# Hash attention and a squared-ReLU layer: the general path's transfers on GpSimd's queue, its flag loaded inside the last output product, and the last block's quarters turned by VectorE alone

## The chip, the cores and the metric

The kernel runs on one core of a Trainium2 chip. The metric is the device time of one execution in microseconds. A core has a matrix engine (TensorE, PE in the profile), three engines for elementwise work (VectorE or DVE, ScalarE or ACT, GpSimd or POOL) and SyncE (SP), which mostly issues transfers. Each engine runs its own queue of instructions in order and waits on semaphores that others raise. DMA queues move data between the main memory (HBM) and the on-chip memory (SBUF); matmuls write to PSUM. SP, ACT and POOL can issue transfers.

## The reference

```python
def _attn_ref(q, k, v, proj):                 # q, k, v: (4, 8, 768, 64), proj: (64, 6)
    scale = 1.0 / np.sqrt(D)
    q_bits = (np.einsum('bhsd,dk->bhsk', q, proj) > 0).astype(np.int64)
    k_bits = (np.einsum('bhsd,dk->bhsk', k, proj) > 0).astype(np.int64)
    powers = 2 ** np.arange(n_bits)
    q_bucket = np.sum(q_bits * powers, axis=-1)
    k_bucket = np.sum(k_bits * powers, axis=-1)
    mask = q_bucket[:, :, :, None] == k_bucket[:, :, None, :]
    scores = scale * np.matmul(q, k.transpose(0, 1, 3, 2))
    scores = np.where(mask, scores, -1000000000.0)
    scores = scores - np.max(scores, axis=-1, keepdims=True)
    attn = np.exp(scores)
    attn = attn / (np.sum(attn, axis=-1, keepdims=True) + 1e-09)
    return np.matmul(attn, v).astype(np.float32)

def _moe_ref(x, w_in, w_out):                 # x: (3072, 512), w_in: (512, 2048), w_out: (2048, 512)
    h = x @ w_in
    r = np.maximum(h, 0.0)
    return ((r * r) @ w_out).astype(np.float32)
```

The attention's heads are joined to 512 features per token and go through the second function. Everything is float32.

## The kernel before

The program has two paths. The **fast path** (up to line 1454) does the whole work without taking the maximum of the scores out first. The **general path** (`general`, line 1459) computes everything again in the safe way, in loops; it is skipped unless the inputs are large. Which it is, is decided by a flag, `slow`: the kernel squares and sums all of q and k in 32 pieces (`load_peak`, `peak`), `tops` (line 886) and `guard` (line 889) take the largest sum, and `guard` writes `slow` (line 895) as 1 if it is over a bound. At the end every engine loads `slow` into a register (line 1488) and branches (line 1489). For the inputs of the metric the flag is 0 and the general path isn't run.

The fast path has two stages. The first does attention, two heads at a time. The second does both weight matrices with a scheme that saves multiplications: a 2x2 block product takes seven products of sums of blocks instead of eight, and it is used twice, one inside the other. Tokens are worked in three chunks of 1024 (`NCHUNK`). Of a chunk, the hidden layer comes first (`hidden`, `hidden_pair`), then `project(i)` (line 1258) makes the output with seven outer products, k = 0 to 6, each of them a call of `product` (line 828).

One call of `product` in `project` is seven groups of four fp32 matmuls (a group is one call of the inner function `add`), over three accumulators in PSUM. The trace shows each of these matmuls as two, so a group is 8 rows. ScalarE copies snapshots of the accumulators to SBUF between the groups (`one`, `two`, `five`, `three`, by `keep`, line 844), and the callbacks c11, c12, c21, c22 combine them on VectorE (line 1199) into blocks of the output. I number the groups 0 to 6 in the order of the code. Group 2 starts in the accumulator of group 0 once `one` has been copied; `two` waits for group 2, `five` for group 3, `three` for group 4; c11 needs group 1, c22 needs `three` and `five`, c12 group 5, c21 group 6. `hook` is called after group 1 and puts VectorE's preparation of later operands there.

The order of the work is that of the code: each engine takes its instructions as the program emits them. `guard` is emitted after the product k = 5 of the last chunk and before the last product, k = 6. Its transpose on PE (line 892) is queued right ahead of group 0 of the last product; its two small VectorE instructions (lines 894, 895) are queued behind all the combining and turning of product 5.

The output's blocks are held with features along the partitions and have to be turned before they are stored. `put_out` (line 1209) turns 32x32 squares on VectorE and stores the block in four transfers with 128 bytes in a run. The last product of the last chunk makes one block row in four quarters, n = 0, 3, 1, 2 in that order (`last` moves c22 ahead of c12), each 128x256. `close` sends quarters 0, 3 and 1 to `put_part` (line 1225): VectorE turns the 32x32 squares, and four transfers of 32 KB go out, two on GpSimd's queue and two on SP's. Quarter 2, the last, goes to `put_last` (line 1240): PE transposes its two 128x128 halves into PSUM, VectorE copies one half and ScalarE the other to SBUF, and each half goes out in one transfer of 64 KB, on SP's and on ScalarE's queue.

After that come the loads of the flag, the branches, and an end section: SP waits for the semaphores of all transfers and engines, and two barriers follow. In the general path all transfers are issued from SP's queue, and two from ScalarE's; the loops over heads, query tiles, batches and so on are real loops with registers.

Of the kernel before, what the change touches and what calls it, by code (L numbers as in the profile page):

```python
# [8 lines left out]
FP32 = mybir.dt.float32  # L9
# [25 lines left out]
def kernel(  # L35
# [10 lines left out]
    nc = tc.nc  # L46
# [3 lines left out]
    NBITS = proj.shape[1]  # L50
    DM = H * D
    DFF = moe_w_in.shape[1]
    P = 128
# [12 lines left out]
    NCH = 1024  # L66
    NCHUNK = B * S // NCH
# [3 lines left out]
    ident = glob.tile([P, P], FP32, name="ident")  # L71
    slow = glob.tile([1, 1], I32, name="slow")
# [584 lines left out]
    with tc.manual_schedule():  # L657
# [166 lines left out]
        )  # L824

        KEPT = dict(one=2, two=1, three=2, five=1)

        def product(n, w, at, bt, c11, c12, c21, c22, hook=None, last=False):

            acc = [ps_m.tile([P, 512], FP32, name=f"acc{i}")[:, 0:w] for i in range(3)]

            def add(to, a, b, first, last):
                for i in range(n):
                    nc.tensor.matmul(  # L837
                        out=acc[to], lhsT=a(i), rhs=b(i), start=first and i == 0,
                        stop=last and i == n - 1, skip_group_check=True,
                    )  # L840

            def keep(of, name):
                t = p_r.tile([P, 512], FP32, name=name, bufs=KEPT[name])[:, 0:w]
                nc.scalar.copy(out=t, in_=acc[of])  # L844
                return t

            add(0, at(0), bt["11"], True, False)
            one = keep(0, "one")
            add(1, at(1), bt["21"], True, True)
            if hook:  # L850
                hook()
            c11(acc[1], one)
            add(0, at(4), bt["t2"], False, False)
            two = keep(0, "two")
            add(2, at(3), bt["t1"], True, False)
            five = keep(2, "five")
            add(0, at(5), bt["t3"], False, False)
            three = keep(0, "three")
            add(2, at(6), bt["22"], False, True)
            if last:  # L860
                c22(three, five)
            c12(acc[2], two)
            if not last:
                c22(three, five)
            add(0, at(2), bt["t4"], False, True)
            c21(acc[0])
# [372 lines left out]

        def put_last(n, o):  # L1240

            row, col = n // 2, n % 2
            ot = p_r.tile([P, HN], FP32, name="h", bufs=NH)[:, 0:QN]
            lo = (NCHUNK - 1) * NCH + col * QN
            for t in range(QN // P):
                at = slice(t * P, (t + 1) * P)
                tp = ps_m.tile([P, 512], FP32, name=f"acc{t}")[:, 0:P]
                nc.tensor.transpose(out=tp, in_=o[:, at], identity=ident)  # L1248
                if t:
                    nc.scalar.copy(out=ot[:, at], in_=tp)  # L1250
                else:
                    nc.vector.tensor_copy(out=ot[:, at], in_=tp)
# [202 lines left out]

    general(tc, slow, ident, w_in_7, w_in_21, w_out_1, q, k, v, proj, out_v)


def general(tc, slow, ident, w_in_7, w_in_21, w_out_1, q, k, v, proj, out_v):


    nc = tc.nc
# [16 lines left out]
    with ExitStack() as stack:  # L1479
# [7 lines left out]
        y_dram = drams.tile([NFF, P, S], FP32, name="y_d")  # L1487
        flag = nc.values_load(slow)
        with tc.If(flag > 0), ExitStack() as inner:
# [3 lines left out]
            for n, f, c in (0, 0, 0), (5, nf, 0), (6, nf, nr):  # L1493
                for i in range(nf):
                    nc.sync.dma_start(
                        out=w_in_d[c:c + nr, :, f + i], in_=w_in_7[:, :, n, i]
                    )
            for i in range(nf):
                nc.sync.dma_start(
                    out=w_in_d[nr:NFF, :, i].rearrange("r p c -> p r c"),  # L1500
                    in_=w_in_21[:, i].rearrange("p (r c) -> p r c", c=P),
                )
            nc.sync.dma_start(out=w_out, in_=w_out_1)
            pool = inner.enter_context(tc.tile_pool(name="g_pool", bufs=1))
# [21 lines left out]
            with tc.For_i(0, B * H, 1) as hd:  # L1526
                nat = []
                for i, src in enumerate(heads):
                    t = pool.tile([P, SB * D], FP32, name=f"g_nat{i}")
                    nc.sync.dma_start(  # L1530
                        out=t, in_=src[bass.ds(hd, 1)].rearrange("o p f -> (o p) f")
                    )
# [17 lines left out]
                )  # L1550
                nc.sync.dma_start(
                    out=ext_dram.rearrange("t r c -> r t c"),
                    in_=ext[0:K, 0].rearrange("r (t c) -> r t c", t=SB),
                )
                with tc.For_i(0, SB, 1) as qt:
                    ext_q = pool.tile([P, P], FP32, name="g_ext_q")
                    nc.sync.dma_start(
                        out=ext_q[0:K], in_=ext_dram[bass.ds(qt, 1)].rearrange("o r c -> (o r) c")
# [29 lines left out]
                    for t in range(SB):  # L1588
# [8 lines left out]
                    )  # L1597
                    nc.sync.dma_start(
                        out=x_dram[bass.ds(hd, 1)][:, bass.ds(qt, 1)].rearrange("o u p d -> (o u p) d"),
# [4 lines left out]
            with tc.For_i(0, B, 1) as b:  # L1604
                with tc.For_i(0, NFT, 1) as j:
                    x_nat = pool.tile([P, SB, 2, D], FP32, name="g_xn")
                    for h in range(2):
                        nc.sync.dma_start(
                            out=x_nat[:, :, h],
                            in_=xs[bass.ds(b * NFT + j, 1), :, :, h].rearrange("o p t d -> (o p) t d"),  # L1610
                        )
                    x_j = pool.tile([P, S], FP32, name="g_xj")
                    turn(x_j, [x_nat[:, t].rearrange("p h d -> p (h d)") for t in range(SB)], P)
                    nc.sync.dma_start(
                        out=xt_dram[bass.ds(j, 1)].rearrange("o p s -> (o p) s"), in_=x_j
                    )
                x_t = pool.tile([P, NFT, S], FP32, name="g_xt")
                nc.sync.dma_start(out=x_t, in_=xt_dram.rearrange("j p s -> p j s"))
                with tc.For_i(0, NFF, 1) as ff:
                    w = pool.tile([P, NFT, P], FP32, name="g_w")  # L1620
                    nc.sync.dma_start(
                        out=w, in_=w_in_d[bass.ds(ff, 1)].rearrange("o p t c -> (o p) t c")
                    )
                    for c in range(2):
                        hp = ps.tile([P, 512], FP32, name="g_hp")
                        for ft in range(NFT):
# [7 lines left out]
                        nc.vector.tensor_tensor(out=r, in0=r, in1=r, op=ALU.mult)  # L1634
                        nc.sync.dma_start(
                            out=y_dram[bass.ds(ff, 1), :, c * HS:(c + 1) * HS].rearrange(
# [4 lines left out]
                with tc.For_i(0, SB, 1) as t:  # L1641
                    gate = pool.tile([P, NFF, P], FP32, name="g_gate")
                    nc.sync.dma_start(
                        out=gate,
# [5 lines left out]
                    for ff in range(NFF):  # L1650
# [5 lines left out]
                    nc.scalar.copy(out=o, in_=y)  # L1656
                    nc.sync.dma_start(
                        out=out_v[bass.ds(b, 1)][:, bass.ds(t, 1)].rearrange("o u p m -> (o u p) m"),
# [31 lines left out]
```

## Time and profile before

| what | us |
|---|---|
| median of 3 runs (lowest, highest) | 860.94 (860.58, 861.04) |
| the profiled execution | 861.34 |
| its span, first to last instruction | 859.6 |
| PE busy | 847.7 |
| VectorE busy | 748.8 |
| ScalarE busy | 401.9 |
| GpSimd busy | 169.0 |
| granted clock of PE, mean of the span | 0.997 |

The span is what the trace shows; 1.74 us of the profiled execution's time lie around it. PE is busy 99% of the span, so the other engines' busy times matter only where PE waits for them. Loads of registers, branches, waits on semaphores and the issuing of transfers aren't counted as busy; they are found in the view of one line's instructions and in the waits of a queue (SPq is SP's queue, PEldq PE's sequencer). Line numbers are those of the kernel before; in the changed kernel the same code stands 1 line (in `product`) to 18 lines further up or down.

### The profile page before, as it was taken

Reading aid. Unit: us, or ns where it says so; the run is one execution under the profiler, and the core shown is the slowest. Engines: PE = TensorE matmul, PEld = TensorE weight load, DVE = VectorE, ACT = ScalarE, POOL = GpSimd, SP = SyncE. Lnnn points to the kernel's source line nnn. Section 1 sums busy time; section 2 is a strip of 40 time slices with the busy share of each in tenths; the row PEclk is TensorE's granted clock in tenths of the full one; section 3 lists DMA queues with packets and bytes.
Section 4 is the critical chain, followed back from the end, with each engine's and each line's share of the span. In section 5 each row is a group of like instructions: output and inputs, shape, how many; then the busy total and the mean of one; then the engine's idle time right before and its main releaser. Section 6 shows DMA issues by size and latency. Waiting matters only on the chain.

```text
span 859.6 us, 17003 instructions
## 1 busy us (share of the span) xinstructions
PE 847.7 (99%) x6593; PEld 528.6 (62%) x6593; DVE 748.8 (87%) x1026; ACT 401.9 (47%) x752; POOL 169.0 (20%) x284
## 2 busy tenths in 40 slices
PE   8999999999999999999999999999999999999996
PEld 3544444444544444444788866567888766668885
DVE  5899999999999987988979978888889788888875
ACT  5787777788877752222111145553111355541110
POOL 1321111123221101643122121111000211100004
PEclk9999999999999999999999999999999999999998
DMA  9677898879998526999977975538557865335565
GB/s 202 134 145 152 175 187 197 198 165 257 246 228 218 169 69 234 326 319 302 346 241 224 268 184 203 182 98 298 174 158 197 178 217 187 122 119 158 159 168 117
DMA packets 235175, 170.15 MB, mean 198 GB/s; under 512 B 168552, under 2 KB 192176, under 8 KB 235088
## 3 DMA queue, kind: packets, MB, share of 16 engines
q1 hardware_dynamic: 195376, 87.85, 41.4%
q0 software_dynamic: 16608, 42.54, 16.1%
q10 hardware_dynamic: 23104, 38.61, 14.8%
q8 instruction: 53, 0.87, 0.4%
q14 instruction: 34, 0.28, 0.1%
HBM read 127.14 MB, written 41.16 MB: 196 GB/s over the span
## 4 chain that ended last, share of the span: by engine, by line
PE 98%; DMA 1%; DVE 0%; ACT 0%; issue 0%; ACTq 0%; DVEq 0%
PE acc L837 41%; PE st L430 18%; PE xo L485 14%; PE acc L1097 13%; PE acc L1050 8%; PE tot L534 2%; PE hash L360 1%; DMA qk_nat<-in_k_dram 1%; ACT e L436 0%; DVE bits L410 0%; PE xo L360 0%; DVE feat L329 0%; PE tp L320 0%; ACTq L284 0%; PE acc L1248 0%
## 5 line engine op out<-in xcount | busy, mean ns | idle before, releaser
L436 ACT ACTIVATE e<-st 128x768 f32<-128x768 f32 x192 | 155.4, 810 | 59.0 <-PE st L430 56.1
L430 PE MATMUL st<-feat 64*64 64x384 f32 x1536 | 157.8, 483 | 1.0 <-DVE feat L329 1.0
L485 PE MATMUL xo<-e,v_nat 64*64 64x385 f32 (+1 forms) x1520 | 157.6, 483 | 0.0
L837 PE MATMUL acc<-b,leaf 128*128 128x256 f32 x600 | 133.2, 379 | 0.4 <-issue 0.4
L837 PEld LDWEIGHTS acc<-b,leaf 128*128 128x128 f32 x600 | 113.8, 190 | 16.8 <-issue 1.3
L473 DVE TENSOR_TENSOR total<-total,e 128x1536 f32<-128x1536 f32 x64 | 111.7, 1745 | 4.2 <-ACT e L436 2.8
L396 POOL DMA_DIRECT2D bits<-signed x120 | 61.9, 520 | 217.8 <-ACT signed L385 199.2
L485 PEld LDWEIGHTS xo<-e,v_nat 64*64 64x64 f32 (+1 forms) x1520 | 57.2, 133 | 66.5 <-issue 57.6
L1097 PE MATMUL acc<-t_x,w_unit 128*128 128x512 f32 x192 | 90.9, 595 | 0.0
L430 PEld LDWEIGHTS st<-feat 64*64 64x64 f32 x1536 | 56.4, 133 | 38.6 <-issue 33.0
L837 PE MATMUL acc<-t,leaf 128*128 128x256 f32 x336 | 76.0, 379 | 0.0
L837 PEld LDWEIGHTS acc<-t,leaf 128*128 128x128 f32 x336 | 63.8, 190 | 8.9 <-issue 0.3
L912 DVE SCALAR_TENSOR_TENSOR b<-h 128x512 f32<-128x512 f32 x96 | 65.7, 691 | 3.0
L430 PE MATMUL st<-bits 64*64 64x384 bf16 x768 | 65.4, 325 | 0.5 <-ACT e L436 0.3
L837 PE MATMUL acc<-x,w_unit 128*128 128x512 f32 x128 | 56.5, 593 | 0.0
L837 PE MATMUL acc<-b_t,leaf 128*128 128x256 f32 x240 | 53.8, 379 | 0.0
L844 ACT COPY two<-acc 128x256 f32<-128x256 f32 (+1 forms) x29 | 12.5, 431 | 87.8 <-PE acc L837 53.8
L1097 PEld LDWEIGHTS acc<-t_x,w_unit 128*128 128x128 f32 x192 | 35.8, 190 | 26.7 <-issue 23.0
L1218 POOL DMA_DIRECT2D out_dram<-h x24 | 15.5, 655 | 182.0 <-DVE h L1213 180.4
L837 PEld LDWEIGHTS acc<-b_t,leaf 128*128 128x128 f32 x240 | 45.5, 190 | 6.3
L844 ACT COPY one<-acc 128x256 f32<-128x256 f32 (+1 forms) x29 | 12.5, 432 | 78.8 <-PE acc L837 64.3
L430 PEld LDWEIGHTS <-bits 64*64 64x64 bf16 x768 | 24.1, 107 | 38.1 <-issue 37.4
(178 smaller groups left out, 1288.9 us busy)
## 6 DMA issues: line engine op xcount, KB each, us to landing
leaf<-w_out ACTq DMA_DIRECT2D x142, 256.0 KB, 3.1
raw<-in_moe_w_in_dram SPq DMA_DIRECT2D x8, 1024.0 KB, 6.9
raw<-in_moe_w_out_dram SPq DMA_DIRECT2D x8, 1024.0 KB, 7.8
w_unit<-w_in SPq DMA_DIRECT2D x16, 512.0 KB, 4.1
w_unit<-w_in SPq DMA_DIRECT2D x8, 896.0 KB, 8.6
w_out<-sums POOLq DMA_DIRECT2D x16, 448.0 KB, 7.6
v_nat<-in_v_dram SPq DMA_DIRECT2D x16, 384.0 KB, 5.2
x_all<-x_t SPq DMA_DIRECT2D x16, 384.0 KB, 3.0
```

Of the source, the lines that this page charges most:

```text
L396: nc.gpsimd.dma_start(out=t[h * D:h * D + NBITS + 1, w, c * HS:(c + 1) * HS], in_=signed[at:at + NBITS + 1, h],)
L430: nc.tensor.matmul(out=st[k * HK:(k + 1) * HK, h, 0:HS], lhsT=src[1][rows, key], rhs=src[0][rows, cut], start=first, stop=not first, skip_ ...
L436: nc.scalar.activation(out=key_of(pr, kt)[:, :, i, 0:HS], in_=st[:, :, 0:HS], func=ACTF.Exp, scale=scale)
L473: nc.vector.tensor_tensor(out=totals[pr], in0=totals[pr], in1=e, op=ALU.add)
L485: return nc.tensor.matmul(out=outs[pr][h * D:(h + 1) * D, c, 0:HS + 1], lhsT=nat[pr, "v_nat"][rows, h, kt * D:(kt + 1) * D], rhs=key_of(pr ...
L534: done = nc.tensor.matmul(out=spares[pr][g * 32:(g + 1) * 32, c2, 0:QS], lhsT=ones[rows], rhs=totals[pr][rows, h, c, c2 * QS:(c2 + 1) * QS ...
L837: nc.tensor.matmul(out=acc[to], lhsT=a(i), rhs=b(i), start=first and i == 0, stop=last and i == n - 1, skip_group_check=True,)
L844: nc.scalar.copy(out=t, in_=acc[of])
L912: nc.vector.scalar_tensor_tensor(out=out, in0=h, scalar=0.0, in1=h, op0=ALU.max, op1=ALU.mult)
L1050: nc.tensor.matmul(out=out, lhsT=w(a), rhs=b, start=start, stop=stop, skip_group_check=True)
L1097: nc.tensor.matmul(out=to, lhsT=w[:, PLACE[a], f], rhs=bt[b](f), start=first and f == 0, stop=last and f == NFT // 2 - 1, skip_group_check ...
L1218: queue.dma_start(out=out[at, m0 + a * 32:m0 + (a + 1) * 32].rearrange("(c i) j -> i c j", i=32), in_=ot[a * 32:(a + 1) * 32].rearrange("i ...
```

## The change

Three things are changed.

1. In the last product, right after c11 (behind group 1 on PE), `nc.values_load(slow)` is called. It puts one load of the flag on the queue of each of the five engines: on PE between groups 1 and 2, on ScalarE ahead of the copy `two`, on VectorE behind the turning of quarter 0, on SP and GpSimd behind the stores of quarter 0. Each load waits until VectorE has written `slow`. The register is handed to `general`, which branches on it and loads no flag of its own.
2. `put_last` and the table `LATE` are gone. All four quarters of the last block go through `put_part`: VectorE turns 32x32 squares, and four transfers of 32 KB go out, two on SP's queue and two on ScalarE's, for quarter 0 on GpSimd's.
3. In `general`, every transfer is issued from GpSimd's queue instead of SP's and ScalarE's.

```diff
+        flags = []
         KEPT = dict(one=2, two=1, three=2, five=1)
@@ product
             c11(acc[1], one)
+            if last:
+                flags.append(nc.values_load(slow))
             add(0, at(4), bt["t2"], False, False)
             two = keep(0, "two")
@@ put_part
-        LATE = {0: (nc.gpsimd, nc.sync), 3: (nc.sync, nc.gpsimd), 1: (nc.sync, nc.gpsimd)}
-
             for a in range(P // 32):
-                LATE[n][a % 2].dma_start(
+                queue = (nc.sync, nc.scalar if n else nc.gpsimd)[a % 2]
+                queue.dma_start(
                     out=out[lo:lo + QN, m0 + a * 32:m0 + (a + 1) * 32].rearrange(
                         "(c i) j -> i c j", i=32
                     ),
                     in_=ot[a * 32:(a + 1) * 32].rearrange("i (c j) -> i c j", j=32),
-                )
-
-        def put_last(n, o):
-
-            row, col = n // 2, n % 2
-            ot = p_r.tile([P, HN], FP32, name="h", bufs=NH)[:, 0:QN]
-            lo = (NCHUNK - 1) * NCH + col * QN
-            for t in range(QN // P):
-                at = slice(t * P, (t + 1) * P)
-                tp = ps_m.tile([P, 512], FP32, name=f"acc{t}")[:, 0:P]
-                nc.tensor.transpose(out=tp, in_=o[:, at], identity=ident)
-                if t:
-                    nc.scalar.copy(out=ot[:, at], in_=tp)
-                else:
-                    nc.vector.tensor_copy(out=ot[:, at], in_=tp)
-                (nc.scalar if t else nc.sync).dma_start(
-                    out=out[lo + t * P:lo + (t + 1) * P, HD + row * P:HD + (row + 1) * P],
-                    in_=ot[:, at],
                 )
@@ close
                 if (i, ih, jh) == (NCHUNK - 1, 1, 0):
-                    put = put_last if n == 2 else put_part
-                    put(n, o[0][:, n % 2 * QN:(n % 2 + 1) * QN])
+                    put_part(n, o[0][:, n % 2 * QN:(n % 2 + 1) * QN])
@@
-    general(tc, slow, ident, w_in_7, w_in_21, w_out_1, q, k, v, proj, out_v)
+    general(tc, flags[0], ident, w_in_7, w_in_21, w_out_1, q, k, v, proj, out_v)
@@ general
-        flag = nc.values_load(slow)
         with tc.If(flag > 0), ExitStack() as inner:
...
-                    nc.sync.dma_start(
+                    nc.gpsimd.dma_start(
                         out=w_in_d[c:c + nr, :, f + i], in_=w_in_7[:, :, n, i]
                     )
...
-                nc.scalar.dma_start(out=projx[:, c * NBITS:(c + 1) * NBITS], in_=proj)
+                nc.gpsimd.dma_start(out=projx[:, c * NBITS:(c + 1) * NBITS], in_=proj)
```

The rest of the diff is the same replacement of `nc.sync.dma_start` in `general` by `nc.gpsimd.dma_start`, thirteen more times.

More of the change, by code (lines that the diff above doesn't have):

```diff
@@ L1454, with general @@
     fast.close()
-    general(tc, slow, ident, w_in_7, w_in_21, w_out_1, q, k, v, proj, out_v)
-def general(tc, slow, ident, w_in_7, w_in_21, w_out_1, q, k, v, proj, out_v):
+    general(tc, flags[0], ident, w_in_7, w_in_21, w_out_1, q, k, v, proj, out_v)
+def general(tc, flag, ident, w_in_7, w_in_21, w_out_1, q, k, v, proj, out_v):
     nc = tc.nc
@@ L1498, in general @@
             for i in range(nf):
-                nc.sync.dma_start(
+                nc.gpsimd.dma_start(
                     out=w_in_d[nr:NFF, :, i].rearrange("r p c -> p r c"),
@@ L1502, in general @@
                 )
-            nc.sync.dma_start(out=w_out, in_=w_out_1)
+            nc.gpsimd.dma_start(out=w_out, in_=w_out_1)
             pool = inner.enter_context(tc.tile_pool(name="g_pool", bufs=1))
@@ L1529, in general @@
                     t = pool.tile([P, SB * D], FP32, name=f"g_nat{i}")
-                    nc.sync.dma_start(
+                    nc.gpsimd.dma_start(
                         out=t, in_=src[bass.ds(hd, 1)].rearrange("o p f -> (o p) f")
@@ L1550, in general @@
                 )
-                nc.sync.dma_start(
+                nc.gpsimd.dma_start(
                     out=ext_dram.rearrange("t r c -> r t c"),
@@ L1556, in general @@
                     ext_q = pool.tile([P, P], FP32, name="g_ext_q")
-                    nc.sync.dma_start(
+                    nc.gpsimd.dma_start(
                         out=ext_q[0:K], in_=ext_dram[bass.ds(qt, 1)].rearrange("o r c -> (o r) c")
@@ L1597, in general @@
                     )
-                    nc.sync.dma_start(
+                    nc.gpsimd.dma_start(
                         out=x_dram[bass.ds(hd, 1)][:, bass.ds(qt, 1)].rearrange("o u p d -> (o u p) d"),
@@ L1607, in general @@
                     for h in range(2):
-                        nc.sync.dma_start(
+                        nc.gpsimd.dma_start(
                             out=x_nat[:, :, h],
@@ L1613, in general @@
                     turn(x_j, [x_nat[:, t].rearrange("p h d -> p (h d)") for t in range(SB)], P)
-                    nc.sync.dma_start(
+                    nc.gpsimd.dma_start(
                         out=xt_dram[bass.ds(j, 1)].rearrange("o p s -> (o p) s"), in_=x_j
@@ L1617, in general @@
                 x_t = pool.tile([P, NFT, S], FP32, name="g_xt")
-                nc.sync.dma_start(out=x_t, in_=xt_dram.rearrange("j p s -> p j s"))
+                nc.gpsimd.dma_start(out=x_t, in_=xt_dram.rearrange("j p s -> p j s"))
                 with tc.For_i(0, NFF, 1) as ff:
                     w = pool.tile([P, NFT, P], FP32, name="g_w")
-                    nc.sync.dma_start(
+                    nc.gpsimd.dma_start(
                         out=w, in_=w_in_d[bass.ds(ff, 1)].rearrange("o p t c -> (o p) t c")
@@ L1634, in general @@
                         nc.vector.tensor_tensor(out=r, in0=r, in1=r, op=ALU.mult)
-                        nc.sync.dma_start(
+                        nc.gpsimd.dma_start(
                             out=y_dram[bass.ds(ff, 1), :, c * HS:(c + 1) * HS].rearrange(
@@ L1642, in general @@
                     gate = pool.tile([P, NFF, P], FP32, name="g_gate")
-                    nc.sync.dma_start(
+                    nc.gpsimd.dma_start(
                         out=gate,
@@ L1656, in general @@
                     nc.scalar.copy(out=o, in_=y)
-                    nc.sync.dma_start(
+                    nc.gpsimd.dma_start(
                         out=out_v[bass.ds(b, 1)][:, bass.ds(t, 1)].rearrange("o u p m -> (o u p) m"),
```

## The prediction

> **What bounds the kernel now.** I read the page's chain of waits first: PE carries 98% of the span, so whatever holds PE is paid in full, and whatever another engine does costs only after PE's last matmul.
>
> ```profile
> PE 98%; DMA 1%; DVE 0%; ACT 0%; issue 0%; ACTq 0%; DVEq 0%
> ```
>
> Then the timeline of the last 20 us, PE alone and then the rows beside it (start, length, engine, line, operation, out<-in, count):
>
> ```profile
> 839.45 3.62 PE L837 MATMUL acc<-b_t,leaf 128*128 128x256 f32 x16
> 842.90 3.62 PE L837 MATMUL acc<-t,leaf 128*128 128x256 f32 x16
> 846.36 5.34 PE L837 MATMUL acc<-b_t,leaf 128*128 128x256 f32 x24
> 852.21 0.44 PE L1248 MATMUL acc<-ident,o 128*128 128x128 f32 x2 [0.51 <-DVE o L1199]
> ```
>
> ```profile
> 844.47 0.71 DVE L1213 STREAM_TRANSPOSE h<-o 128x512 f32<-128x512 f32 x1
> 845.10 0.24 DVE L894 TENSOR_REDUCE most<-tp 1x1 f32<-1x128 f32 x1
> 845.37 0.14 DVE L895 TENSOR_SCALAR slow<-most 1x1 int32<-1x1 f32 x1
> ...
> 851.74 0.42 DVE L1199 TENSOR_TENSOR o<-sum,acc 128x256 f32<-128x256 f32 x1 [0.36 <-PE acc L837]
> 852.58 0.29 DVE L1252 COPY h<-acc 128x128 f32<-128x128 f32 x1 [0.42 <-PE acc L1248]
> ```
>
> The last product is the 56 matmul rows of PE from 839.45: seven groups of 8, 12.1 / 7 = 1.73 us each. Group 1 (the second) is done and group 2 starts at 842.90. VectorE is behind: it writes `slow` at 845.37 + 0.14 = 845.51, **2.6 us after PE went on to group 2**. Nothing on PE waits for `slow` today. PE ends at 851.70, the span at 859.6: a tail of 7.9 us. What fills it is in the view of one line's instructions (the load of the flag, L1488; the branch, L1489) and in the waits of SP's queue:
>
> ```profile
> L1488 PEldq TENSOR_LOAD <-slow x1: 487/487/487, 852.2 to 852.2; - x1
> L1488 DVEq TENSOR_LOAD <-slow x1: 645/645/645, 852.6 to 852.6; - x1
> L1488 SPq TENSOR_LOAD <-slow x1: 516/516/516, 853.3 to 853.3; - x1
> ...
> L1489 SPq EVENT_SEMAPHORE  x8: 17/17/17, 857.4 to 857.9; - x8
> ```
>
> ```profile
> SPq L1489 <- SPq L1489: 3.4, 1, 3.4
> ```
>
> SP issues the last store at 852.9, loads the flag, branches at 853.9 over the untaken general path and runs nothing for 3.4 us. No transfer explains it: the last stores issue at 852.90 and 852.98 and need 3.5 and 3.6 us to land (view of L1253), so they are down by 856.5, while SP's first check, of a transfer that landed earlier, comes at 857.4. PE, DVE and ACT go on 0.4 to 0.5 us after the same branch. In the built program SP jumps 269 instructions, POOL 156, ACT 169, DVE 189. The page's queue of instruction loads for these four (q14) carries 0.28 MB in 34 packets, 8.2 KB each; all instruction packets together are 1.15 MB for 17,003 instructions, 68 bytes each, so a packet is some 120 instructions. I read SP's 3.4 us as a jump past what had been loaded, with a load to wait for.
>
> **The change, part by part.**
>
> *Flag loaded early.* The load on PE now stands between groups 1 and 2 and waits for `slow`. PE's queue is in order: in the trace PE's load, whose flag had been there since 845.51, ran only at 852.21, when the weight load ahead of it was released. So groups 2 to 6 are queued behind it, and VectorE, ScalarE and the stores behind those. Price: flag 845.51, load 0.49, 0.1 to the next instruction (the gap between PE's load and its branch), weights 0.2: group 2 starts at 846.35 instead of 842.90, **+3.45 us**. If the load lets the next instruction pass, 845.75, +2.85; the order of rows says it holds, so I take 3.45. The flag cannot come sooner: VectorE's rows from 837.88 to 845.51 stand back to back, and the diff moves nothing ahead of L895. The other four loads are hidden: ACT's 0.60 lies before the copy `two`, which waits 3.1 us for PE; DVE's 0.65 before `tmp` of quarter 3, which waits 0.77 us for a copy, and longer after the stall; SP's 0.52 and POOL's 0.54 before a store not due for 1.3 us, or before nothing.
>
> *PE's clock.* PE then idles from 843.1 to 846.35, 3.25 us. This trace has no such gap. The rows nearest to it (columns: stretch, length, PE busy, PEld, DVE, ACT, POOL, granted clock, DMA share, GB/s):
>
> ```profile
> 850.65:854.06 3.41, 1.49 (x7) 0.77 (x5) 1.40 (x4) 0.27 (x1) 2.01 (x4) 1.00 0.63 106
> 854.06:857.40 3.34, 0.00 (x0) 0.00 (x0) 0.00 (x0) 0.00 (x0) 0.00 (x0) 0.50 0.10 25
> ...
> 4.14:7.56 3.42, 2.34 (x15) 1.21 (x14) 0.00 (x0) 0.86 (x2) 0.00 (x0) 1.00 1.47 167
> ```
>
> The records have full clock from 4.14 to 854.06, 249 times 3.413 us, so it is decided on a fixed grid. After a stretch with PE busy 1.49 of 3.41 us (44%) it was halved; after one with 2.34 (68%) it was not. A gap of 3.25 us puts at least 1.6 us of idling into one stretch, so that stretch is at most 52% busy; on this grid (843.82 to 847.23) 26%. I expect half clock for one stretch: of 0.9 to 1.7 us of lost work, by where the grid falls, I take **+1.6**; ends 0 and 3.4 (two stretches).
> The Trainium skill, "TensorE: Matmul & The Clock Gate", Part 1, says that the clock halves after at least one idle window of about 3.4 us, free-running. The grid agrees with the trace; the 44% row speaks against "idle". By the Trainium skill's wording a gap of 3.25 us fills no window, and the sum would lack the 1.6.
>
> *The tail.* Removed: PE's two transposes (0.44), both copies, all five flag loads, POOL's four late stores. Added: VectorE's transpose of 128x256, 0.45 (L1229). With PE's end still at 851.70: `o` to 852.17, transpose to 852.66 (today's copies end at 852.87 and 852.96). Then two stores each on SP and ACT, 0.32 and 0.45 to issue. SP's second shares a semaphore with ACT's first store of quarter 1 (issued about 851.4, landing 1.8 later), so it goes at 853.25, ends 853.7 and lands at 855.05, by the 1.8 us of the median of such SP stores. SP jumps at 853.75, over 169 instructions instead of 269: as ACT did over 169 in 0.5 us. After the landing come what is left of the semaphore checks and the barrier, 1.2 us in today's rows (858.4 to 859.6). End 856.25; 0.3 more for instruction loads of other engines in the way (I put today's 3.5 us of the last stores down to them: five such packets in 853.5 to 855.8), 856.6: **-3.0 us**. Bounds: -3.3, and -0.8 if SP still waits for instructions.
> The Trainium skill, "Runtime: NRT & Kernel Launch", Instruction fetch mechanics, has a taken branch out of a two-block window wait for a load, as I read SP's row; its blocks are 256 instructions, against the 120 of q14 here. With its blocks SP's 269 would mostly be inside, the 3.4 us would be something else, and the sum would be about 2 us higher.
>
> *General path on GpSimd's queue.* None of it runs; it moves code. POOL's jump grows from 156 to 234, between 189 (quick) and 269 (3.4 us). POOL branches near 849, its last stores issuing at 848.2 and 848.8; 3.4 us ends near 852.5, and its 2.25 us drain (L1686) still ends before SP's checks. Cost nothing; without that cover at most 3.4.
>
> **Sum**, against the profiled execution (span 859.6, 861.34 with what lies around it): 3.45 + 1.6 - 3.0 = +2.05, 863.4. The median of the three runs, 860.94, is 0.4 lower: **863.0**.
>
> **Rivals.**
> 1. *The clock stays.* The 44% stretch was the last with any matmul, so it may have been halved for what came after it and not for its share; then a gap that ends before the stretch does would leave the clock alone. Against it: the halving came at that stretch's end, 1.4 us after the last matmul. 3.45 - 3.0 = +0.45: 861.4. Chance 0.11.
> 2. *SP still waits for instructions.* The shorter jump may land just ahead of a block's end, so that the next block is needed at once, or the 3.4 us has another cause. Then the gain is 0.8 to 1.1: 3.45 + 1.6 - 1.0 = +4.05, 865.0. For it: the end section's 17 instructions must all fit; against it: three engines jumped as far without a wait. Chance 0.22.
> 3. *Faster: PE isn't held.* If `slow` is written before PE reaches the load, 2.6 us earlier than in the profiled execution, or if PE runs past the load's wait, only the tail is left: -3.0, 857.9. It decides at 842.9, the start of group 2. Against it: VectorE has no gap in the 7.6 us before. Chance 0.05.
> 4. *Half clock for two stretches.* +1.7 more: 864.7. Chance 0.05.
>
> **How the numbers follow.** The forecast has 0.57; with the clock's phase (0.9 to 1.7) and the landing it spreads from 862.0 to 863.9. A measurement of this kernel can tell about 0.2%, 1.7 us, from no change: slower begins at 862.66, within the forecast (0.36 slower, 0.21 same). Slower: 0.36 + 0.22 + 0.05 + 0.01 (a part of rival 1) = 0.64; same: 0.21 + 0.10 = 0.31; faster: rival 3, 0.05. The range takes in rivals 1, 2 and 4 and leaves out rival 3 and the far ends: 861.2 to 865.4.
>
> **What would show it.** Stall: PE idle just ahead of group 2 for about 3.2 us, ended by `slow`, with VectorE idle before `tmp` of quarter 3. Clock: 0.50 in one 3.41 us stretch of the last product, its matmuls 0.43 us apart instead of 0.22. Tail: from PE's end to the span's end 4.9 us instead of 7.9, SP's checks starting within 0.5 us of its branch. Wrong if group 2 starts before 845, if the granted clock stays 1.00, or if SP shows 3 us without an instruction again.

## The result and the profile after

The changed kernel took **864.52 us** in the median of 7 runs (863.01 to 865.59), the kernel before 861.04 on the same chip (860.58 to 861.97): ratio 1.0038, interval 1.0027 to 1.005. It is slower by 3.5 us, from median to median; the ratios here and below are not quotients of the medians and can differ from them a little. The profiled execution took 864.5 us with a span of 862.9 us, 3.3 more than before.

The chain of waits of the kernel after, by engine, has lost 1% of PE to others:

```profile
PE 97%; DVE 1%; DMA 1%; issue 0%; ACT 0%; DVEq 0%
```

The timeline of its last product, PE and VectorE (start, length, engine, line, operation, out<-in, count, and idle time with what ended it):

```profile
840.62 3.62 PE L838 MATMUL acc<-b_t,leaf 128*128 128x256 f32 x16
...
846.54 0.14 DVE L898 TENSOR_SCALAR slow<-most 1x1 int32<-1x1 f32 x1
...
847.98 3.69 PE L838 MATMUL acc<-t,leaf 128*128 128x256 f32 x16 [3.74 <-DVE b_t L593]
...
851.50 5.34 PE L838 MATMUL acc<-b_t,leaf 128*128 128x256 f32 x24
...
853.84 0.42 DVE L1202 TENSOR_TENSOR tmp<-three,five 128x256 f32<-128x256 f32 x1 [4.75 <-ACT three L845]
...
857.34 0.45 DVE L1230 STREAM_TRANSPOSE h<-o 128x256 f32<-128x256 f32 x1
```

Group 2 starts 7.36 us after group 0 (847.98 - 840.62); before it was 3.45 (842.90 - 839.45). PE lost **3.91 us** there. `slow` is written at 846.68, 6.07 us after group 0, exactly as before (845.51 - 839.45 with rounding): the flag isn't later, PE waits for it. The 3.74 in brackets are put down to `b_t`, which VectorE runs right behind `slow`; but group 2 doesn't need it, since in the kernel before it started at 842.90 and `b_t` only at 845.44. The view of the load's line shows what held PE:

```profile
L855 ACTq TENSOR_LOAD <-slow x1: 1010/1010/1010, 846.7 to 846.7; - x1
L855 PEldq TENSOR_LOAD <-slow x1: 1041/1041/1041, 846.7 to 846.7; - x1
```

PE's load starts 0.04 us after the flag is there and takes 1.04 us, twice what it took at the end of the kernel before; the first matmul follows 0.22 us later. VectorE has nothing to do meanwhile (4.75 us idle before `tmp` of quarter 3).

At the other end the tail, from PE's end to the span's end, is 6.05 us (856.85 to 862.90) where it was 7.88. The views of the branch's line and of the end section's line show SP's part:

```profile
L1471 POOLq EVENT_SEMAPHORE  x4: 17/43/43, 853.3 to 853.5; - x4
L1471 POOLq COMPARE_BRANCH  x1: 58/58/58, 850.5 to 850.5; - x1
...
L1471 SPq COMPARE_BRANCH  x1: 50/50/50, 859.0 to 859.0; - x1
```

```profile
L1668 SPq EVENT_SEMAPHORE  x14: 17/28/28, 859.5 to 862.8; - x14
...
L1668 SPq DRAIN  x3: 7/13/130, 861.2 to 862.3; - x3
```

SP's first check comes 0.44 us after its branch; the 3.4 us without an instruction are gone from there. POOL has such a hole now (850.5 to 853.3), hidden. But SP has a new, smaller hole inside its end section: its first drain is done at 861.20 and the second starts at 861.95.

By spans: +1.17 us are there before the last product begins, mostly from a gap of PE at 460 us, where the code is the same (1.96 us here, 0.42 before, and from under 0.2 to 1.39 in the traces of the runs below, an ordinary difference between executions); +3.91 for the gap; -1.83 for the tail. That is 3.25 of the 3.3. The granted clock stayed 1.00 to PE's end in this execution.

### The profile page after: what moved, and what is told of

Read it like the earlier page. It is cut to its first block, busy times and chain, and to the rows that moved or that the text cites. A ratio compares the mean times of both kernels' runs of the same rounds, so it can differ in the third digit from the quotient of the medians.

```text
span 862.9 us, 16994 instructions
## 1 busy us (share of the span) xinstructions
PE 847.9 (98%) x6591; PEld 528.1 (61%) x6591; DVE 749.4 (87%) x1026; ACT 401.9 (47%) x751; POOL 167.2 (19%) x280
## 4 chain that ended last, share of the span: by engine, by line
PE 97%; DVE 1%; DMA 1%; issue 0%; ACT 0%; DVEq 0%
PE acc L838 40%; PE st L430 18%; PE xo L485 14%; PE acc L1100 13%; PE acc L1053 8%; PE tot L534 2%; PE hash L360 1%; DMA qk_nat<-in_q_dram 1%; DVE o L1202 0%; DVE h L1216 0%; PE tp L320 0%; DVE b_t L593 0%; DVE bits L410 0%; DVE sum L1202 0%; ACT feat L327 0%
```

## The experiments

Theory: PE's wait for the flag costs 3.9 us in each execution, and in most of them the clock is halved as well; SP's shorter jump gives part of it back. Twelve runs follow; the kernel before, run beside them, had medians of 861.0 to 861.3 us.

### The flag loaded where it is ready (late_load)

```diff
@@ product of the changed kernel
-            if last:
-                flags.append(nc.values_load(slow))
             add(0, at(4), bt["t2"], False, False)
...
             add(2, at(6), bt["22"], False, True)
             if last:
+                flags.append(nc.values_load(slow))
                 c22(three, five)
```

> The changed kernel with one line moved: the flag is loaded behind group 5 of the last product instead of behind group 1, when the flag has long been written. If the loss is PE waiting for the flag (3.9 us of idling ahead of group 2 in the profile after, 1.8 us given back by the tail), this should be faster than the kernel before by about 1.8 us, near 859.2, with no idle PE in the last product. If the loss comes from the new way to turn and store the last quarter, or from the code moved to GpSimd, it should stay at 863 or more.

Measured: 861.34 us, ratio 1.0003 (0.9994 to 1.0012). The gap is gone in PE's timeline, group 2 starts 3.46 us after group 0:

```profile
838.84 3.62 PE L838 MATMUL acc<-b_t,leaf 128*128 128x256 f32 x16
842.30 3.62 PE L838 MATMUL acc<-t,leaf 128*128 128x256 f32 x16
```

So **the wait for the flag, with what it does to the clock, is the whole loss**; moving one statement removes it. But the gain in the tail has gone with it: 7.68 us from PE's end, though SP's first check still comes 0.44 us after its branch. SP branches late, 3.99 us after PE's end. Two of the waits of its queue from 840 us on (engine and line, what ended the wait, us in total, times, longest):

```profile
SPq L1234 <- DMA out_dram<-h: 2.2, 2, 1.8
SPq L1234 <- DVE h L1229: 2.1, 2, 1.9
```

The 1.8 us is a wait for a transfer, not for data. In these traces the transfers of SP's and ScalarE's queues signal their landing on the same 8 semaphores, and in the built program of this kernel quarter 1's first store on SP has the semaphore of quarter 1's first store on ScalarE. Its data is there at 850.77, and it is issued at 852.91, when ScalarE's has landed.

### The early load alone (early_only)

The kernel before with the first part of the change only.

> The kernel before with the early load of the flag alone; last quarter and general path as before. If the stall is the loss: plus 3.9 us of idle PE, minus some 0.5 us of flag loads that leave the tail, so near 864.5, up to 866 where PE's clock is halved for a stretch after the gap; SP's 3.4 us without an instruction stays. If the other two edits make the loss: 861, as before.

Measured: 866.25 us, ratio 1.0059 (1.0047 to 1.0071), a little over what I expected. Group 2 is 3.81 us late, and in its trace the clock is halved for two stretches, 844.35 to 851.17, another 2.85 us (13 matmuls at 0.43 us in place of 0.22). The tail keeps SP's 3.33 us.

### The general path's transfers alone (general_only)

The kernel before with the third part only.

> The kernel before with the general path's transfers moved to GpSimd's queue, nothing else. If SP's 3.4 us after its branch is a load of instructions past a long jump, it is gone, and SP is held by the last stores' landing (856.5 in the profile before) instead: the span ends near 858, about 1.5 us sooner, 859.5. If these 3.4 us have another cause, the time stays at 861. GpSimd's own jump becomes long; if its load of instructions comes late, it could take SP's place, and the time would stay at 861 too, with the wait on GpSimd.

Measured: 860.84 us, ratio 0.9999 (0.9988 to 1.0011). SP's jump is short, the time is the same. The view of the branch's line tells why:

```profile
L1489 POOLq EVENT_SEMAPHORE  x4: 17/43/43, 856.0 to 856.3; - x4
L1489 POOLq COMPARE_BRANCH  x1: 58/58/58, 853.2 to 853.2; - x1
...
L1489 POOLq INC_SWDGE_SEM  x1: 707/707/707, 856.4 to 856.4; - x1
```

**The hole has moved from SP to POOL** (853.2 to 856.0, SP idle with it until 857.0), with POOL's last semaphore instruction behind it, 0.7 us, which I read as the settling of the skipped transfers' semaphores, and POOL's drain, 2.2 us, which ends at 859.3; SP has been waiting since 857.9. In the full change POOL branches 6.4 us ahead of PE's end instead of 1.0 us behind it, since it has no late stores and PE is held, and all this is hidden.

### The full change with the flag loaded at the end (end_load)

> The changed kernel with the flag loaded at its old place, behind everything. If the stall is the loss, near late_load: 859.2, since a load of 0.5 us and a branch on SP lie beside the 1.9 us in which the last stores land. If an early load is worth something in the tail, it is slower than late_load by up to 1 us, because each engine's jump comes later.

Measured: 862.02 us, ratio 1.0009 (1.0 to 1.0017), tail 8.67 us. As in late_load, SP's stores wait for ScalarE's on the same semaphores; SP branches 5.20 us after PE's end. It is 0.7 us slower than late_load, in median, and the intervals overlap: that an early load is worth something in the tail is not shown.

### The change once more (after_again)

> The changed kernel itself, on the chip of the next three kernels, for a second trace. Theory A (stall of 3.9 us always; in a part of the executions the clock is halved for one or two stretches of 3.41 us as well, by where the grid falls): +2 us over the kernel before in executions with full clock, +3.7 to +5.4 in the others, so a median of +3 to +4 (ratio 1.0035 to 1.0047) and single times spread over some 3 us. Theory B (the stall alone, the clock never): +2.1 us (ratio 1.0024) and a spread like that of the kernel before. Tail from PE's end to the span's end 6.0 us in both.

Measured: 865.1 us (862.05 to 867.04, 7 runs), ratio 1.0037 (1.0021 to 1.0054). Its trace is that of the longest run, and there the clock did fall. PE's timeline of it comes first, then the stretches of the clock's grid around the gap, of after_again and, in the last fence, of the first trace (stretch, length, PE, PEld, DVE, ACT and POOL busy, granted clock, DMA share, GB/s):

```profile
840.04 3.62 PE L838 MATMUL acc<-b_t,leaf 128*128 128x256 f32 x16
847.50 6.70 PE L838 MATMUL acc<-t,leaf 128*128 128x256 f32 x16 [3.84 <-DVE b_t L593]
```

```profile
843.35:846.76 3.41, 0.31 (x2) 0.00 (x0) 3.27 (x8) 0.00 (x0) 1.87 (x4) 1.00 0.84 174
846.76:850.17 3.41, 2.67 (x6) 2.19 (x7) 1.69 (x4) 0.00 (x0) 3.03 (x5) 0.50 0.92 127
850.17:853.59 3.42, 3.42 (x9) 2.70 (x8) 0.00 (x0) 0.37 (x1) 0.00 (x0) 0.50 0.24 43
```

```profile
842.78:846.20 3.42, 1.46 (x7) 0.95 (x5) 3.28 (x8) 0.14 (x1) 2.33 (x4) 1.00 0.99 194
846.20:849.61 3.41, 1.63 (x8) 1.48 (x9) 2.79 (x7) 0.00 (x0) 2.81 (x5) 1.00 0.99 129
```

The same gap, cut differently by the grid. In after_again it fills one stretch (PE busy 0.31 us, 9%), and the next two run at half clock: groups 2 and 3 take 6.70 us instead of 3.62. In the first trace it is shared by two stretches (43% and 49% busy), and nothing happens. The 14 times of the changed kernel fit: four with a mean granted clock of 0.998 or 0.999 at 862.05, 862.17, 863.01 and 864.5 (the profiled one, which lost 1.17 us earlier), ten with 0.995 to 0.997 at 864.41 to 867.04.

The Trainium skill, "TensorE: Matmul & The Clock Gate", Part 1, has the clock halved after an idle window of about 3.4 us and full again after one sustained busy one. The traces agree with the second (2.67 us of PE in a stretch did not restore it, 3.42 did); "idle" must be read loosely, since 0.31 us of matmuls did not prevent the halving.

### The gap filled with work (filled, filled_7)

```diff
@@ product of the changed kernel
             if last:
+                for i in range(14):                  # filled; 7 in filled_7
+                    nc.tensor.matmul(out=acc[2], lhsT=at(3)(i % n), rhs=bt["t1"](i % n),
+                                     start=True, stop=True, skip_group_check=True)
                 flags.append(nc.values_load(slow))
```

> The changed kernel with 14 needless matmuls (128x256, into a PSUM buffer that group 3 starts afresh) put between group 1 and the load of the flag, so that PE is busy for 3.0 of the 3.9 us in which it idled. They give group 2 no earlier start: it still waits for the flag. Theory A: the time falls to that of the stall with full clock, some 863.0 (+2 over the kernel before), 1 to 1.7 us under the changed kernel on the same chip, with less spread, and the trace shows 1.00 to PE's end. Theory B: the same time as the changed kernel within 0.5 us. If the load runs only behind the 14 matmuls, up to 0.8 us more in either.

Measured: 866.21 us, ratio 1.0069 (1.0055 to 1.0083), 3 us over the forecast. A miss of mine in the size: each call is two rows, so the filling was 28 rows, 6.05 us, longer than the gap. PE's end comes exactly 6.05 us later after group 0 than before (18.30 against 12.25), with the clock at 1.00.

> As the run filled, but with 7 needless calls, 14 rows of 0.216 us or 3.02 us (the 14 calls of filled were 28 rows, 6.05 us, more than the gap). PE is busy for 3.0 of the 3.9 us and group 2 still waits for the flag. Theory A (the clock is halved after the gap in a part of the changed kernel's executions, which makes the difference between its times near 862.1 and those of 864.4 to 867): group 2 starts 3.7 to 4.1 us late, the clock stays 1.00 to PE's end in every execution, no single time above 864, a median of 862.5 to 863.3, ratio 1.0018 to 1.0026, where the changed kernel had 1.0037. Theory B (the later times of the changed kernel have another cause): its spread and median stay, 864.5 to 865. If the load waits until the 14 rows are through, up to 0.5 us more in either.

Measured: 863.38 us (862.1 to 864.17, 8 runs), ratio 1.0025 (1.0015 to 1.0035), granted clock 0.998 to 1.0 in every run. PE's timeline:

```profile
840.27 3.62 PE L838 MATMUL acc<-b_t,leaf 128*128 128x256 f32 x16
843.72 3.19 PE L856 MATMUL acc<-t,leaf 128*128 128x256 f32 x14
847.33 3.69 PE L838 MATMUL acc<-t,leaf 128*128 128x256 f32 x16 [0.42 <-issue]
```

Group 2 starts only 0.3 to 0.4 us earlier (7.06 us after group 0, against 7.36 and 7.46), and **needless matmuls made the kernel faster**, by keeping the clock up: +2.1 us over the kernel before instead of +3.5 and +4.1. The intervals of the ratios overlap, but the single times hardly do: none of the eight is over 864.17, and eleven of the changed kernel's fourteen are. Of the difference, 1.4 to 2.0 us between medians, some 0.5 is the earlier group 2 and a slightly shorter tail (5.91); that leaves about 0.9 to 1.5 us as an estimate of the clock's price over many executions. Theory B is out.

### The flag computed earlier (guard_early)

```diff
-                if k == 5 and i + 1 == NCHUNK:
+                if k == 4 and i + 1 == NCHUNK:
```

(The line that emits `guard`; the loads stay where the change has them.)

> The changed kernel with the flag computed one product earlier (VectorE's reduction and comparison 12 us sooner); the loads stay between groups 1 and 2. Theory A (the loss is the wait for the flag, not the load): PE has no gap over 0.5 us, the clock stays, and because the built program gives SP's stores the same semaphores as in late_load the tail is 7.5 to 7.9: 861.0 to 861.6, ratio 1.000 to 1.0007. Rival (a load on PE in the midst of the product costs by itself, 0.5 to 1.0 us): 861.8 to 862.6.

Measured: 861.95 us, ratio 1.0006 (0.9998 to 1.0015). That median lies in the rival's range and not in theory A's; the trace decides. PE's timeline, and then the load's line:

```profile
840.12 3.62 PE L838 MATMUL acc<-b_t,leaf 128*128 128x256 f32 x16
843.57 3.62 PE L838 MATMUL acc<-t,leaf 128*128 128x256 f32 x16
847.02 5.34 PE L838 MATMUL acc<-b_t,leaf 128*128 128x256 f32 x24
```

```profile
L855 PEldq TENSOR_LOAD <-slow x1: 484/484/484, 839.7 to 839.7; - x1
```

Groups 0, 2 and 4 follow without a gap: a load on PE in the midst of a product cost nothing with the flag there. The load stands behind group 1 but ran before group 0's first matmul, as PE's sequencer works ahead of the matmuls that are queued (by 2.8 us in late_load, where the load ran at 846.40 and group 5, ahead of it, ended at 849.2), and so its 0.48 us are hidden. What is over theory A's range is the tail, 8.02 us instead of 7.5 to 7.9, with the stores' semaphores as in late_load.

### The long jump put back (late_sp)

late_load with the general path's transfers on SP's queue again.

> The flag loaded ahead of the last group, VectorE's transposing and the new queues of the stores kept, but the general path's transfers back on SP's queue, so that SP's jump is the long one again. Theory A (SP's wait comes from the length of the jump): SP runs nothing for 2.8 to 3.4 us after its branch (0.45 with the short jump), and then goes through its end section without another hole; from branch to SP's last drain 4.2 to 4.9 us in place of 2.74, so 1.5 to 2.1 us more than with the short jump: 862.8 to 863.5, ratio about 1.002. Rival (something other than the jump's length decides): no change against the short jump, 861.3.

Measured: 863.0 us, ratio 1.0028 (1.0017 to 1.0038): 2.0 us over the kernel before on its chip, where late_load is 0.2 over. The hole behind the branch is back in SP's waits, and the one inside the end section is gone:

```profile
SPq L1470 <- SPq L1470: 2.6, 1, 2.6
```

From its branch to its last drain ahead of the barriers SP takes 4.04 us (2.74 in late_load); the tail is 9.44. So the hole goes with the long jump. A packet of instructions on q14 (8 KB) starts 0.9 us after SP's branch and is through at 857.05, and the first check comes 1.2 us later; whose packet it is, the records don't say. The rule in the Trainium skill, "Runtime: NRT & Kernel Launch", Instruction fetch mechanics, that a taken branch out of what is loaded waits for a load, agrees.

### Trying for a better kernel (late_fewer, mixed, mixed_2)

late_fewer: late_load with quarter 3's stores on SP and GpSimd.

> The flag loaded ahead of the last group (no stall), and quarter 3's second and fourth stores on GpSimd's queue, as in the kernel before; only quarters 1 and 2 have stores on ScalarE's queue. Theory A (without the stall SP's last stores came late because 12 stores of three quarters go round 8 semaphores, each free only when its earlier store has landed): 10 stores go round, SP's last store issues some 1.8 us after PE's end in place of 3.5, SP branches at +2.2, the next block of instructions is there 2.7 us later, +4.9, the barrier ends at +5.9; GpSimd's jump (2.8 us) and drain now begin 1.2 us later and may end at +6.4. Tail 5.9 to 6.4 in place of 7.7, 859.3 to 859.8, ratio 0.998 to 0.9985. Rival (the stores are late for another reason, such as the landing of the transfers themselves): tail 7.5 to 7.9 and 861.

Measured: 861.41 us, ratio 1.0011 (1.0002 to 1.0019), tail 7.76. **My count of stores was the wrong idea**: with two fewer, quarter 1's two stores on SP still have the semaphores of quarter 1's two on ScalarE, and wait for them to land (the first is issued at 853.33, its data is there at 851.11).

mixed: late_load with the kernel before's `put_last` for quarter 2, quarter 1's four stores on SP.

```diff
+        LATE = {0: (nc.gpsimd, nc.sync), 3: (nc.sync, nc.gpsimd), 1: (nc.sync, nc.sync)}
```

> A candidate for a better kernel: the flag loaded ahead of the last group (no stall), the general path on GpSimd's queue (SP's short jump), quarters 0 and 3 on SP's and GpSimd's queues, quarter 1 on SP's alone, and the last quarter turned by PE with one store each on SP and ScalarE as in the kernel before. In the built program no late store is given a semaphore that a store of the same or the preceding quarter holds. Theory A (the tail of the late_load kernel lost 1.8 us because SP's stores waited for ScalarE's stores on the same semaphores): SP's last store issues 1.3 to 1.5 us after PE's last product ends, branch at +1.9 to 2.1, next block of instructions 2.5 to 2.95 us after the branch, span's end at +5.8 to +6.3 in place of 7.7 to 7.9: 859.3 to 859.8, ratio 0.998 to 0.9986. Rival (the landing of the last stores, 3.5 us, or GpSimd's jump and drain takes the place): tail 6.8 to 7.9, 860.3 to 861.3.

Measured: 860.41 us, ratio 0.9996 (0.9987 to 1.0006), tail 7.51, the rival's time, but from a cause that neither theory had. SP's last store starts in time, 1.68 us after PE's end, without a wait for a semaphore, but the issue itself lasts 1.97 us. The transfers' records show a load of instructions on queue q8 from 853.05 to 854.67, 1.10 us after PE's branch; the issue ends 0.42 us later. In ten traces, eleven such loads have a store issue of SP or ScalarE under way when they end, and each time it ends 0.34 to 0.42 us after the load. In the kernel before, PE branches later, and q8's load (853.91) finds no store left to issue.

mixed_2: mixed, and PE's branch 0.7 us later.

```diff
@@ end of put_last
+            tp = ps_m.tile([P, 512], FP32, name="acc2")[:, 0:P]
+            nc.tensor.transpose(out=tp, in_=ot[:, 0:P], identity=ident)
```

> The kernel mixed with one needless transpose on PE behind its last two, which waits for VectorE's last copy, so that PE's branch comes 0.7 us later; nothing else waits for it. In mixed SP's last store issued in time (853.12, 1.7 us after PE's last product) but the issue itself took 1.97 us, and ended 0.42 us after PE's instruction load (queue q8, 853.05 to 854.67, 1.1 us after PE's branch). Theory A (a load of PE's instructions holds SP's and ScalarE's issues of stores until 0.4 us after it): now it comes behind the last issue, which takes 0.35 us; SP branches at about +2.1 after the last product in place of +3.7, the next block 2.5 to 2.95 us after it, tail 5.7 to 6.5 in place of 7.5: 858.9 to 859.7, ratio 0.9975 to 0.9985. Rival (the long issue has another cause, such as the store's own size or a full queue): the issue is long again, tail 7.3 to 7.9, 860.4 to 861.

Measured: 860.75 us, ratio 0.9995 (0.9986 to 1.0004), tail 7.05. The view of the last stores' line, of mixed (SP's store) and then of mixed_2:

```profile
L1255 SPq DMA_DIRECT2D out_dram<-h x1: 1973/1973/1973, 853.1 to 853.1; - x1
```

```profile
L1255 ACTq DMA_DIRECT2D out_dram<-h x1: 352/352/352, 853.9 to 853.9; - x1
...
L1255 SPq DMA_DIRECT2D out_dram<-h x1: 395/395/395, 854.4 to 854.4; - x1
...
DMA to landing us min/median/max: 3.4/3.5/3.6
```

The long issue is gone (0.40 us), as expected, and SP branches 2.22 us after PE's end. Yet the rival's time came out: now the landing ends last. SP's queue waits for the last stores, 2.0 us at the longest:

```profile
SPq L1689 <- DMA out_dram<-h: 2.6, 2, 2.0
```

Their packets travel while five instruction loads run (854.7 to 856.4). That these loads make the landing late is not shown. Neither version can be told from the kernel before.

The tails side by side, us from PE's last product:

| kernel | SP branches | branch to SP's last drain ahead of the barriers | to the span's end | tail | what SP waits for last |
|---|---|---|---|---|---|
| before | 2.19 | 4.88 | 0.81 | 7.88 | 3.41 behind the branch |
| after | 2.15 | 2.95 | 0.95 | 6.05 | 0.75 in the end section |
| general_only | 2.18 | 3.44 | 2.29 | 7.91 | POOL |
| late_load | 3.99 | 2.74 | 0.95 | 7.68 | 1.21 in the end section |
| late_sp | 4.59 | 4.04 | 0.82 | 9.44 | 2.57 behind the branch |
| mixed | 3.71 | 2.98 | 0.82 | 7.51 | 1.10 in the end section |
| mixed_2 | 2.22 | 4.00 | 0.83 | 7.05 | landing |

## Why the prediction was right, and where its sizes were off

The direction and the range held: 863.0 (861.2 to 865.4) against 864.52. The likeliest case was spread over 862.0 to 863.9; the median lies 0.6 us above that, where the range took in rivals 2 and 4. Of the signs of being wrong one came in the profiled execution: the granted clock stayed 1.00 to PE's end. By its steps:

- **Stall, +3.45: right, 0.46 short** (3.91 in the profiled execution, 4.01 and 3.81 in the other two traces with the stall). That PE's queue is held by the load, that the flag comes no sooner, and the writing of the flag 6.07 us after group 0 all came as put. The term that was mis-sized is the load, 1.04 us and not 0.49 (and the terms as listed give 846.30, +3.40). ScalarE's load runs in the same microsecond (1.01), but in late_sp, mixed and mixed_2 ScalarE's comes only after PE's is done, and PE's still takes 1.03 to 1.07. There VectorE's load begins 0.49 us into it; in guard_early PE's is alone and takes 0.48, but in the kernel before it takes 0.49 with GpSimd's beside it for 0.44 us. What lengthens it stays open.
- **Clock, +1.6: about right as a mean, not as one execution.** I expected one stretch; the traces show none and two. One is likely among the others: two halved stretches, 6.83 us, take an execution's mean clock to 0.996 or less, the profiled one without any has 0.998, and five of the fourteen have 0.997. This is an estimate, no trace shows one. The rule I took from one row, that a gap leaving a stretch at 52% or less halves the clock, was too wide: stretches at 43% and 49% were followed by full clock. The row I took it from (1.49 us busy) held 0.44 us of transposes; without them it is 1.05 us, 31%. If such transposes don't count, which no run tests, the rows of these runs put the line for matmuls between 1.05 and 1.46 us of a stretch. So rival 1 (the clock stays) and rival 4 (two stretches) are both what happens, by the phase of the grid.
- **Tail, -3.0: -1.83.** SP's jump went as put: 0.44 us. What failed is "after the landing come what is left of the semaphore checks": the end section isn't all loaded. In rival 2 I had a next block needed "at once"; it is needed 13 instructions later, and is there only 2.5 to 2.95 us after the branch in after, late_load, end_load, late_fewer and guard_early. The place supports that it is a block's end: in mixed, where SP's program is one instruction longer, the hole is one instruction earlier. So the floor from SP's branch is 2.5 to 2.95 us, not the half microsecond and the landing. SP's last store landed late too, 4.01 us after PE's end instead of 3.35; but SP's checks were through at 4.35 and the block came at 5.10, so the block set the end.
- **What I didn't see: this gain needs the stall.** Where PE isn't held, the tail is 7.05 to 9.4 in every version. I had read one shared semaphore off the changed program (SP's second store, put at 1.55 us after PE's end, measured 1.77); which stores share one changes with the planned order, and in late_load the same code loses 1.8 us to it. So rival 3, PE not held, would have given about 861.3 by late_load, not 857.9.
- **GpSimd's queue, nothing: right**, and the cover matters as said: uncovered, POOL's jump and drain set the end in general_only, 1.5 us behind SP.
- **Sum:** +2.05 forecast for the profiled execution, with 1.6 of clock; measured +2.08 without clock (3.91 - 1.83). That these agree is luck: the two misses of size, 0.46 and 1.17, took the place of the 1.6. The median adds the clock's share over the executions, some 1.4, and the two misses are nearly all of the 1.5 us between 863.0 and 864.52.

## What to carry to other kernels

A load of the flag is a wait on every engine that gets it, and on the engine that sets the time it must stand behind work that outlasts the flag: four groups further down it cost nothing here. An idle gap near 3.4 us is priced by how the clock's grid cuts it, so price it as a mean of cases, and ask several executions rather than one trace; filling it with any matmuls is a cheap test. A saving in the tail is worth only the distance to the next thing that ends there, and here five different ones stood within 1 us: SP's jump, POOL's jump, shared semaphores of transfers, PE's instruction load in the way of store issues, and the landing.

## What the runs showed of the hardware that I had not expected

- A load of a 4-byte flag took 0.48 to 1.36 us. The Trainium skill, "DMA: Bandwidth & Descriptors", Latency and other measured facts, gives a floor of about 600 ns; 0.48 is below it.
- A load of instructions on q8 (16 KB, 1.0 to 2.1 us after PE's branch, in filled a second one after 4.1) holds store issues of SP and ScalarE until 0.34 to 0.42 us after its end. That q8 is PE's is inferred from when it comes, and from its moving with PE's branch in mixed_2.
- Halved after a stretch with 0.31, 0.82, 0.85 or 0.97 us of PE in 3.41, not after 1.46, 1.50 or 1.63; once halved, only a stretch busy throughout ended it (2.21 and 2.67 us did not).
- After a long jump nothing ran for 2.57 to 3.41 us behind the branch, on SP and on POOL alike (2.75 and 2.79 on POOL), and the block behind the end section's first instructions came 2.5 to 2.95 us after it (3.8 in mixed_2, where SP had waited for a landing first). That instructions were being loaded meanwhile is inferred from the jump's length and from q14's packets, which start 0.9 to 1.3 us after these branches; in the kernel before SP went on only 2.0 us after the last of them, and what passed then stays open.
